# Lightning attention into a SwiGLU block: the load of the decay bases moves from the sync queue to GpSimd's queue

## The chip, the cores and the metric

The kernel runs on one core of a Trainium2 chip. The metric is device time in microseconds (us) of one launch; the median of three runs before the change is 216.38 us (216.28 to 216.65).

The engines are named as in the profile: PE is TensorE (PEld its weight loads), DVE is VectorE, ACT is ScalarE, POOL is GpSimd, SP is SyncE. A name with a q (SPq, ACTq) is an engine's own queue of instructions that issue DMA transfers or handle semaphores. Each engine works through its instructions in order, and waits on semaphores that other engines or DMA transfers raise.

## What is computed

Linear attention with a decay per head, over blocks of 64 positions, and then a SwiGLU feed-forward block on the result. Shapes: q, k and v are 4 x 8 x 768 x 64 (batch, heads, sequence, head size), lam has 8 values (one decay base per head), the weights are 512 x 1536 twice and 1536 x 512.

```python
def _attn_ref(q, k, v, lam):
    ...
    Dmask = np.where(rel >= 0, lam[:, None, None] ** rel[None, :, :], 0.0)
    lam_pow = lam[:, None, None] ** (pos[None, :, None] + 1)
    lam_block = lam ** block
    ...
    for b in range(nb):
        ...
        intra = np.einsum('bhic,bhjc->bhij', qb, kb) * Dmask[None]
        intra = np.einsum('bhij,bhjd->bhid', intra, vb)
        inter = np.einsum('bhid,bhde->bhie', qb * lam_pow[None], kv_state)
        out[:, :, sl] = intra + inter
        ...
        kv_state = lam_block[None, :, None, None] * kv_state + np.einsum('bhsd,bhse->bhde', kb_dec, vb)

def _moe_ref(x, w_gate, w_val, w_out):
    g = x @ w_gate
    silu = g * (1.0 / (1.0 + np.exp(-g)))
    val = x @ w_val
    return silu * val @ w_out
```

## The kernel before

The work is cut into 12 groups. A group is one batch entry and 256 positions of all 8 heads; two groups make one of six column tiles of the feed-forward part. Per group the kernel loads k, q and v, casts k and q to bf16, transposes them, forms scores, masks them, and multiplies with v; a state per batch entry is carried on. The feed-forward part takes gate and value products over twelve slices of the hidden size (`ffn_gate`, `ffn_val`), and then the output product. The order of all instructions on each engine is written out by hand (`manual_schedule`); a plan attaches the attention work of later groups to steps of the feed-forward loop. So the first two groups stand alone at the head of the kernel, and from the first `ffn_gate` on PE has feed-forward products to work on.

What matters here is the head. The decay bases enter as follows:

- Line 137 loads lam into `lam_row`, one partition of 8 values, as the first transfer of the sync queue.
- Lines 138 to 143 load groups 0 and 1, through `load_fp32` (line 115): k and q in halves of 4 heads (256 KB each), taken in turn, then v in halves. All go to the sync queue, but for the two halves of q of group 0, which ACT's queue issues. After them the sync queue issues the first weights (`w_piece`, line 241).
- On POOL, `make_identity`, two position tables (`irow`, line 159, and `ipos`, line 164) and the causal masks (lines 168 to 179) are built.
- On PE, four filler products into an unused bank (line 188) are followed by line 189, a product of a row of ones with `lam_row`, which puts lam on all 128 partitions. Four more fillers follow (line 154, called at line 190), and then the transposes.
- ACT takes the logarithm of that (lines 201 and 203); DVE multiplies it with `ipos` (line 205), and ACT makes the tables of decays for the queries (`qdec_table`, line 209) before and between its casts of k (line 306), and exponentiates DVE's product (line 945). The casts of q of group 0 are on DVE (line 306 too).
- POOL scales v with these decays (`v_scale`, line 266), and casts a part of group 1.
- Masked scores are made at line 369 on DVE after the score products (line 362) on PE; line 324 (ACT) and line 328 (DVE) take the transposed k and q out of their banks, q with its decays multiplied in.

In the text, k0a and k0b are the two halves of k of group 0, k1a and k1b those of group 1, and q and v likewise.

```python
lam_ps = bank()
b = bank()
for _ in range(4):
    nc.tensor.matmul(b, warm[:, 0:128], warm, start=True, stop=True)
nc.tensor.matmul(lam_ps[:, 0:H], ones[:, 0:128], lam_row, start=True, stop=True)
warm_up(4)
```

Of the kernel before, what the change touches and what calls it, by code (L numbers as in the profile page):

```python
# [19 lines left out]
@with_exitstack  # L20
def kernel(
    ctx: ExitStack,
    tc: tile.TileContext,
    q: bass.AP,
    k: bass.AP,
    v: bass.AP,
    lam: bass.AP,
    moe_w_gate: bass.AP,
    moe_w_val: bass.AP,
    moe_w_out: bass.AP,  # L30
    out: bass.AP,
):
    nc = tc.nc
    with tc.manual_schedule():
        _body(ctx, tc, nc, q, k, v, lam, moe_w_gate, moe_w_val, moe_w_out, out)


def _body(ctx, tc, nc, q, k, v, lam, moe_w_gate, moe_w_val, moe_w_out, out):
    B, H, S, D = q.shape
# [94 lines left out]
                                ap=[[D, n], [-S * D if rev else S * D, H], [1, D]]))  # L134

    lam_row = const.tile([1, H], FP32, name="lam_row")
    nc.sync.dma_start(out=lam_row, in_=bass.AP(tensor=lam.tensor, offset=lam.offset, ap=[[0, 1], [1, H]]))
    for g in range(2):
        for c in range(2):
            load_fp32(g, nc.sync, k, "kraw", c * H // 2, (c + 1) * H // 2)  # L140
# [1149 lines left out]
```

## Time and profile before

| | |
|---|---|
| median of the runs | 216.38 us |
| span of the profiled execution | 215.0 us |
| PE busy | 208.1 us (97%) |
| DVE, ACT, POOL busy | 148.3, 130.9, 92.7 us |
| DMA: moved, mean rate | 39.76 MB, 185 GB/s |
| DMA in the first 14 us | 3.97 MB, 284 GB/s |

The span goes from the first to the last instruction of one profiled execution; the time of a run has some more around it. Busy time is the time in which an engine's instructions run, without those that only issue transfers or handle semaphores. A DMA transfer has two times: that of its issue, which is an instruction of a queue, and that until its data have landed. The profile gives the second only as a figure per group of issues.

The transfers of the first 14 us, as the profile's list of issues has them: the halves of k, q and v are 256 KB, with 4.5, 3.6 (ACT's queue) or 4.5 (SP's), and 4.7 us as the median from issue to landing; for `lam_row` it gives no time to landing.

### The profile page before, as it was taken

What the parts mean: (1) busy time and instruction counts of PE and PEld (TensorE: products, weight loads), DVE (VectorE), ACT (ScalarE), POOL (GpSimd) and SP (SyncE); (2) the same over time, 40 slices, a digit from 0 to 9 for tenths busy, and PEclk for the clock granted to TensorE, in tenths of its full rate; (3) what the DMA queues carried; (4) which work ended last, traced back from release to release, by engine and by line L of the source; (5) the groups of instructions that cost most, each with busy time, mean ns of one, the idle gap of its engine ahead of it and who ended that gap; (6) DMA issues with size and microseconds to landing.
All of it is one profiled execution on the core that took longest, in us unless ns stands there. A gap on an engine that the chain in (4) does not pass through costs nothing.

```text
span 215.0 us, 6856 instructions
## 1 busy us (share of the span) xinstructions
PE 208.1 (97%) x2797; PEld 153.3 (71%) x2801; DVE 148.3 (69%) x267; ACT 130.9 (61%) x280; POOL 92.7 (43%) x128
## 2 busy tenths in 40 slices
PE   8789999999999999999999999999999999999993
PEld 3467445887888548866754545888888888888883
DVE  1773447576677989874569878697988389961940
ACT  5878676756636153638369487774983676636522
POOL 6675755818399440595962153240750022200200
PEclk9999999999999999999999999999999999999999
DMA  6999999999999778899576859855000500005014
GB/s 188 345 354 381 376 336 296 285 226 223 309 387 174 185 212 208 244 214 263 122 198 143 217 121 257 207 121 201 5 3 5 195 0 3 0 0 198 0 52 146
DMA packets 82176, 39.76 MB, mean 185 GB/s; under 512 B 45410, under 2 KB 77794, under 8 KB 82146
## 3 DMA queue, kind: packets, MB, share of 16 engines
q1 hardware_dynamic: 80946, 38.74, 64.7%
q10 hardware_dynamic: 1200, 0.59, 0.9%
q8 instruction: 22, 0.36, 0.7%
q14 instruction: 8, 0.07, 0.1%
HBM read 28.31 MB, written 6.29 MB: 161 GB/s over the span
## 4 chain that ended last, share of the span: by engine, by line
PE 93%; DMA 2%; DVE 1%; SPq 1%; ACT 0%; issue 0%; DVEq 0%
PE bank L823 22%; PE bank L585 20%; PE bank L603 19%; PE bank L733 17%; PE bank L623 5%; PE bank L531 3%; DMA kraw<-in_k_dram 2%; PE bank L518 2%; PE bank L424 2%; PE bank L362 1%; DVE ssb L369 1%; SPq L115 1%; PE bank L392 1%; PE bank L322 1%; ACT qk L306 0%
## 5 line engine op out<-in xcount | busy, mean ns | idle before, releaser
L607 DVE TENSOR_TENSOR h<-sil,bank 128x256 bf16<-128x256 bf16 (+1 forms) x67 | 35.0, 533 | 29.9 <-PE bank L603 17.2
L585 PE MATMUL bank<-xt,wg_sb 128*128 128x256 bf16 (+1 forms) x276 | 52.8, 315 | 0.0
L603 PE MATMUL bank<-xt,wv_sb 128*128 128x256 bf16 (+1 forms) x276 | 52.5, 314 | 0.0
L590 ACT ACTIVATE sil<-bank 128x256 bf16<-128x256 f32 (+1 forms) x67 | 31.6, 481 | 21.8 <-PE bank L585 18.4
L603 PEld LDWEIGHTS <-wv_sb 128*128 128x128 bf16 x276 | 26.9, 98 | 14.8 <-POOL wv_sb L249 0.2
L585 PEld LDWEIGHTS <-wg_sb 128*128 128x128 bf16 x276 | 25.9, 98 | 13.6 <-issue 0.2
L266 POOL TENSOR_TENSOR v_s<-v,dec 128x512 bf16<-128x512 f32 (+1 forms) x18 | 23.0, 1295 | 24.3 <-DMA v<-in_v_dram 17.3
L763 POOL TENSOR_TENSOR h<-sil,es 128x512 bf16<-128x512 bf16 x6 | 7.0, 1165 | 47.4 <-ACT sil L760 47.4
L823 PEld LDWEIGHTS <-h 128*128 128x128 bf16 x240 | 23.3, 98 | 3.4 <-issue 0.3
L823 PE MATMUL bank<-wo_sb,h 128*128 128x256 bf16 x180 | 21.5, 273 | 0.0
L823 PEld LDWEIGHTS <-hs 128*128 128x128 bf16 x180 | 17.6, 98 | 2.7
L369 DVE TENSOR_TENSOR ssb<-bank,causal 128x512 bf16<-128x512 f32 x24 | 15.4, 684 | 1.8 <-PE bank L362 1.8
L479 POOL TENSOR_TENSOR kvf<-kvs,ups 128x256 f32<-128x256 f32 x8 | 6.5, 814 | 20.9 <-ACT ups L446 20.9
L733 PEld LDWEIGHTS <-ws 128*128 128x128 bf16 x144 | 13.8, 98 | 1.8
L823 PE MATMUL bank<-wt,hs 128*128 128x256 bf16 x120 | 15.0, 273 | 0.0
L775 DVE TENSOR_TENSOR bank<-bank,es 128x512 f32<-128x512 f32 x12 | 7.8, 694 | 9.6 <-PE bank L733 9.6
L479 POOL TENSOR_TENSOR kvf<-kvf,ups 128x256 f32<-128x256 f32 x16 | 13.0, 815 | 0.9
L760 ACT ACTIVATE sil<-bank 128x512 bf16<-128x512 f32 x18 | 10.5, 596 | 3.7 <-PE bank L733 3.7
L733 PE MATMUL bank<-xs,ws 128*128 128x256 bf16 x96 | 12.6, 273 | 0.0
L763 DVE TENSOR_TENSOR h<-sil,bank 128x512 bf16<-128x512 bf16 x18 | 11.8, 683 | 0.3 <-ACT sil L760 0.3
L623 PE MATMUL bank<-wo_sb,h 128*128 128x512 bf16 x45 | 10.7, 380 | 0.2
L733 PE MATMUL bank<-xt,wg_sb 128*128 128x256 bf16 x72 | 10.8, 273 | 0.0
(119 smaller groups left out, 360.3 us busy)
## 6 DMA issues: line engine op xcount, KB each, us to landing
out_dram<-osb SPq DMA_DIRECT2D x22, 256.0 KB, 2.6
v<-in_v_dram SPq DMA_DIRECT2D x18, 256.0 KB, 4.6
woraw<-in_moe_w_out_dram SPq DMA_DIRECT2D x6, 512.0 KB, 7.1
kraw<-in_k_dram SPq DMA_DIRECT2D x24, 128.0 KB, 3.4
qraw<-in_q_dram SPq DMA_DIRECT2D x24, 128.0 KB, 3.4
wraw<-in_moe_w_gate_dram SPq DMA_DIRECT2D x5, 512.0 KB, 6.9
wraw<-in_moe_w_val_dram SPq DMA_DIRECT2D x5, 512.0 KB, 7.0
kraw<-in_k_dram SPq DMA_DIRECT2D x4, 512.0 KB, 6.3
```

The source lines that it names most:

```text
L266: eng.tensor_tensor(out=st[("vs", g)][:, h0:h1], in0=st[("v", g)][:, h0:h1].rearrange("p h (s d) -> p h s d", s=2), in1=vfac(g, h0, h1), o ...
L369: nc.vector.tensor_tensor(out=ssb[:, h2, 2 * c:2 * c + 2].rearrange("p a s n -> p a (s n)"), in0=sp[(c, h2)].rearrange("p (a x) -> p a x", ...
L479: nc.gpsimd.tensor_tensor(out=o, in0=f, in1=u, op=ALU.add)
L585: nc.tensor.matmul(gp[:, n0:n1], wg_sb[:, mc, fs], xt[:, g0:g1, mc].rearrange("p g b n -> p g (b n)"), start=(mc == 0 and n0 == 0), stop=( ...
L590: nc.scalar.activation(sil[:, 0:N], gp[:, 0:N], AF.Silu)
L603: nc.tensor.matmul(vp[:, n0:n1], wv_sb[:, mc, fs], xt[:, g0:g1, mc].rearrange("p g b n -> p g (b n)"), start=(mc == 0 and n0 == 0), stop=( ...
L607: nc.vector.tensor_tensor(out=h_sb[:, fc % FH, b0:b1].rearrange("p b n -> p (b n)"), in0=sil[:, 0:N], in1=vp[:, 0:N], op=ALU.mult)
L623: nc.tensor.matmul(ps, st[("h", t, fc // FH)][:, fc % FH, b], wo_sb[:, fc, c0:c1], start=(fc == 0), stop=(fc == FC - 1))
L733: nc.tensor.matmul(o[:, fi * 256:fi * 256 + 256], lhs(i, c, 2 * j + fi), rhs(c), start=(start and fi == 0 and c == 0), stop=(c == KH - 1), ...
L760: nc.scalar.activation(sil[key], src, AF.Silu)
L763: eng.tensor_tensor(out=h_of(half, r), in0=v3(sil[half, r]), in1=v3(src), op=ALU.mult)
L823: nc.tensor.matmul(o, lhs(f), rhs(f), start=(start and f == 0), stop=(f == FH - 1), skip_group_check=True)
```

## The change

One word: the load of `lam_row` is issued by GpSimd in place of the sync engine.

```diff
     lam_row = const.tile([1, H], FP32, name="lam_row")
-    nc.sync.dma_start(out=lam_row, in_=bass.AP(tensor=lam.tensor, offset=lam.offset, ap=[[0, 1], [1, H]]))
+    nc.gpsimd.dma_start(out=lam_row, in_=bass.AP(tensor=lam.tensor, offset=lam.offset, ap=[[0, 1], [1, H]]))
```

On POOL the new issue stands ahead of the memset of the identity, the first instruction of the kernel proper there. The sync queue begins with k0a. The number and order of the instructions on PE, DVE and ACT stay as they are.

## The prediction

> **What bounds the kernel now.** I read the page's busy table and slices first, then the chain of waits over the first 30 us, then the timelines of ACT and POOL there, then stretches of DMA rate.
>
> ```profile
> PE 208.1 (97%) x2797; PEld 153.3 (71%) x2801; DVE 148.3 (69%) x267; ACT 130.9 (61%) x280; POOL 92.7 (43%) x128
> PE   8789999999999999999999999999999999999993
> ```
>
> TensorE has work almost all the time; the only slices with holes are the first four, so a change to the loads at the start can move the end only by moving the moment when TensorE becomes solid. From there on everything shifts as a block. The chain of waits (start, length, what):
>
> ```profile
> 0.81 0.35 SPq L137
> 1.16 0.06 issue
> 1.22 0.42 SPq L115
> ...
> 3.33 5.23 DMA kraw<-in_k_dram
> 8.56 0.02 issue
> 8.58 0.63 ACT qk L306
> ...
> 14.72 0.64 PE bank L531 x31
> 15.36 0.54 PE bank L585 x4
> ```
>
> By this chain the head is the SP queue's issues one after another, lam first, then the transfer of the first half of group 1's k (k1a below; q1a, v0a and so on likewise), then its cast on ACT, from which the transposes, scores and masks run to 14.72 and the gate matmuls at 15.36. Lam costs SP 0.35 + 0.06 = 0.41 us there. But a chain shows one path only; ACT's timeline (start, length, engine, line; in brackets the idle time before and its releaser) shows the second:
>
> ```profile
> 3.27 0.18 ACT L201 ACTIVATE ln_lam<-bank 128x8 f32<-128x8 f32 x1 [0.16 <-PE bank L189]
> 3.77 0.91 ACT L209 ACTIVATE qdec<-irow,lnp 128x256 bf16<-128x256 f32 x2
> 4.88 0.62 ACT L306 CAST qk<-kraw 128x512 bf16<-128x512 f32 x1 [0.20 <-DMA kraw<-in_k_dram]
> 7.80 0.57 ACT L324 COPY qkt<-bank 128x512 bf16<-128x512 bf16 x1
> 8.58 0.62 ACT L306 CAST qk<-kraw 128x512 bf16<-128x512 f32 x1 [0.21 <-DMA kraw<-in_k_dram]
> ```
>
> Lam goes through the matmul L189 (start 2.64, when the four fillers of L188 are through; 0.59 long), the logarithms, two exponentials (to 4.68) and only then comes the first cast of k. ACT waited for k only 0.20 at 4.88 and 0.21 at 8.58. So the lam path runs beside the k path with 0.41 us to spare, once L189 is pushed off 2.64.
>
> How early lam lands today: the semaphore event of L189 in the timeline of its line stands at 2.0.
>
> ```profile
> L189 PEldq EVENT_SEMAPHORE  x1: 51/51/51, 2.0 to 2.0; - x1
> 0.80 0.20 POOL masks.py:197 MEMSET ident<- 128x128 bf16 x1 [0.29 <-POOLq L1274]
> 7.23 2.05 POOL L266 TENSOR_TENSOR v_s<-v,dec 128x512 bf16<-128x512 f32 x2 [2.96 <-ACT qk L306]
> ```
>
> If that event is lam's (L189 waits for lam and for the ones of L150, which were there at 1.06), lam needs 1.2 us from its issue at 0.81, 0.84 of it after the 0.35 of issuing, on DMA engines that were still empty. In any case it was there by 2.64. The two POOL lines (start, length) show where the new issue goes, ahead of the identity at 0.80, and how much idle time POOL has before 7.23.
>
> **The change, part by part.**
>
> SP loses one issue: all later issues may start 0.41 earlier. How much of that becomes data is read from the DMA engines (columns of busy time, then clock, DMA share, GB/s):
>
> ```profile
> 2.00:2.50 0.50, 0.50 (x2) 0.00 (x0) 0.00 (x0) 0.50 (x1) 0.50 (x4) 1.00 0.48 108
> 2.50:3.00 0.50, 0.50 (x3) 0.36 (x2) 0.00 (x0) 0.50 (x1) 0.45 (x3) 1.00 0.99 295
> 5.00:5.50 0.50, 0.24 (x4) 0.01 (x1) 0.00 (x0) 0.50 (x2) 0.00 (x0) 1.00 1.15 345
> ```
>
> Full rate is 345 GB/s. In 2.0 to 2.5 the engines are half empty, as only ACT's q is flowing: 0.5 x (345 - 108) = 118 KB missing, 0.34 us at full rate. With k beside q from the start that hole can be filled; after it the engines are full and SP issues at their pace (q1a's issue took 1.70, the next ones come every 0.74 us, 256 KB each, 354 GB/s), so nothing more comes of the 0.41. k1a can land 0 to 0.41 earlier; I take 0.34. q1a also loses its wait for lam's semaphore, which had long passed at 3.88: nothing.
>
> ACT's side allows that much: k0a lands earlier too, the 0.20 of waiting goes, and the rest follows, so ACT is ready for k1a at 8.38 - 0.20 = 8.18, against 8.56 - 0.34 = 8.22 for k1a. The gain with lam in time is therefore 0.34: 216.38 - 0.34 = 216.04.
>
> POOL gains one issue before its tables. The trace has no transfer issued by POOL. Bounds of the issue: 0.35, what SP needs for the same one, and 2.05, the pair of v scalings, as the longest stretch POOL spends on one thing in the head. POOL casts 128x512 f32 in 0.61 where DVE takes 0.43, so POOL is the slower engine for like work and I go above SP: 1.05, one 128x512 scaling. The delay on POOL costs nothing by itself: identity (done 1.37, used 4.74), irow (1.70, used 3.77), ipos (2.06, used 3.55), masks (4.28, used 7.16) each stand an added 1.05; ipos would be late from 1.49 on, and then by the excess, into L205 and the q cast behind it on DVE. POOL's own next work is at 7.23.
>
> Lam's landing, L: 0.80 + issue + flight. Flight is 0.84 on empty engines. Now the engines fill from 2.0 on with k and q. What landing under load adds: from 2.00 to 8.56 they moved 320 GB/s x 6.56 = 2.10 MB, while k1a and all issued before it are 7 x 0.262 = 1.835 MB, so k1a landed some 0.77 after the last byte that it could wait for (an estimate from these rows). I take the whole of it, because lam arrives when both queues are full: L = 0.80 + 1.05 + 0.84 + 0.77 = 3.46, and 0.05 for the semaphore event: 3.5. Bounds: 0.80 + 0.35 + 0.84 = 2.0 (as today), and 0.80 + 5.2 = 6.0, if lam took as long as k1a's 5.23.
>
> What is queued behind the wait: on PE, L189 is followed by the four fillers of L154 (1.75) and by the first transposes; ACT's L201, L203 and L209 hold the first k cast behind them; DVE's L205 holds the cast of q0a. All of them move by 3.5 - 2.64 = 0.86. Of this 0.20 goes into ACT's wait for k0a and 0.21 into that for k1a; the rest, 0.45, is on the path: ACT reaches k1a at 8.38 + 0.66 = 9.04 instead of 8.58. DVE's masks have the same slack (0.46 idle ahead of L328 at 10.68). That k1a lands 0.34 earlier is then worth nothing.
>
> **Sum.** The profiled execution's span is 215.0, 1.4 below the median of the runs, 216.38; this difference stays. +0.45 on the span: 215.45; on the median 216.83, and I say 216.85, +0.2%. A change below 0.2% (0.43 us) can't be told from none, and this forecast sits at that edge: L = 3.47 is the point where it is passed.
>
> **The rivals.**
>
> Covered (not slower): lam lands before 2.8, as in 2.0 plus some tenths, L189 starts within 0.2 of 2.64 and the filled hole brings 0.34: 216.04. For it: L has 0.6 us behind the fillers of L188 today. Against it: one instruction more on a slower engine and full DMA engines. It decides while L is below 2.64 + 0.41 - 0.34 = 2.7 fully, and up to 3.05 in part. The Trainium skill (DMA: Bandwidth & Descriptors, Latency and other measured facts) gives the first byte of a transfer issued by GpSimd at about 1 us and by the sync queue at about 0.6, so 0.4 later; added to 2.05 this would be L = 2.45, hidden, and the time 216.04. No run so far shows it; the page's figure says nothing of full engines.
>
> Wash: L between 2.8 and 3.45, or k1a not earlier because its engines are full anyway: between -0.2 and +0.4, say 216.4.
>
> Clock (slower still): 512-wide fillers start 0.43 apart at L188 and L154 (3.16 to 4.42) though the granted clock reads 1.00, and the same width later takes 0.216 (L585, four in 0.86); PE turned fast near 4.7, after 3.9 us of nearly unbroken work. With a hole of 0.8 us between L188 and L189 this may come later. On the path between 5.56 and 7.60 PE has L322 (0.40), L362 (0.42) and L322 (0.62); at half rate at most 1.44 more, of which I take 1.0: 217.85. It decides if the hole is enough to put off the fast state. Against it: PE stays fast from 5 to 9 with far larger holes. The Trainium skill (TensorE: Matmul & The Clock Gate, Part 1) says that the clock opens after one busy window of about 3.4 us that runs freely, not with the kernel; by it a hole of 0.8 in one window may or may not count.
>
> More than the hole: k1a earlier by the full 0.41 and by the thin 2.5 to 3.0 as well (0.07): 215.9, faster by over 0.2%. It needs lam before 2.7 and ACT ready at 8.1.
>
> **How the numbers follow.** Lam late by POOL's issue and full engines, with 0.43 or more lost: 0.40; its own range is 216.6 to 217.5 (L from 3.3 to 4.2). Clock: 0.10. Wash: 0.22. Covered: 0.20. More than the hole: 0.08. So slower 0.50, same 0.42, faster 0.08. The range reaches from 216.0 (covered) to 217.9 (clock); L above 4.5, and the fast rival, are left out.
>
> **What would show it.** In the new trace: SP's first k issue at about 0.81; the 2.0 to 2.5 stretch near 300 GB/s; L189 starting well after 2.7 with PE idle before it (right), or at 2.64 (covered); ACT's idle time before L306 gone at 4.9 and 8.6 and L306 starting near 9.0; POOL's tables about 1 us later with no one waiting; fillers of L154 and transposes at the old spacing (clock wrong). The forecast falls if L189 still starts at 2.64, or if k1a's cast starts before 8.5.

## The result, and the profile after

The changed kernel takes 222.12 us (median of six; the kernel before 216.36 us beside it), and the ratio is 1.0237, interval 1.0206 to 1.0269. A second set gave 221.57 against 216.41, 1.025 (1.0214 to 1.0287). Slower, as forecast, but by some 5 us where 0.45 was forecast, and outside the range. One of the twelve executions of the two sets had a mean granted clock (the share of full speed that TensorE was given) of 0.57 and took 359.85 us; the ratios leave it out, and what is shown below comes from an undisturbed one, whose span is 219.5 us against 215.0 before.

The page of the changed kernel, busy times and TensorE's slices:

```profile
PE 208.9 (95%) x2797; PEld 154.3 (70%) x2801; DVE 149.0 (68%) x267; ACT 130.8 (60%) x280; POOL 91.6 (42%) x129
...
PE   3986999999999999999999999999999999999993
```

The busy times are the same within 1.1 us; TensorE's slices differ in the first four alone, the first and the fourth having larger holes. So the place to read is the head again. The chain of waits of the changed kernel over the first 24 us (start, length, what):

```profile
1.31 4.51 DMA lam_row<-in_lam_dram
5.82 0.14 issue
5.96 0.56 PE bank L189 x2
6.51 1.82 PE bank L154 x4
8.33 0.43 PE bank L322 x4
...
11.97 0.63 ACT qk L306
...
16.82 1.30 DVE ssb L369 x2
18.12 1.24 issue
19.36 0.64 PE bank L531 x31
20.00 0.54 PE bank L585 x4
```

Before, this chain ran through SP's issues and k1a. Now it begins with lam's transfer, and everything in the head hangs on it: L189 starts at 5.96 instead of 2.64 (+3.32), and by the chain the gate matmuls of L585 at 20.00 instead of 15.36 (+4.64). The span grew by 4.5, so the rest of the kernel moved nearly as a block. Two parts make up the 4.64: the masks (L369) end 3.40 later (18.12 instead of 14.72), and then PE stands for 1.24 us more, marked issue. ACT's timeline of the changed kernel (idle time before and its releaser in brackets):

```profile
6.55 0.18 ACT L201 ACTIVATE ln_lam<-bank 128x8 f32<-128x8 f32 x1 [3.32 <-PE bank L189]
...
7.06 0.91 ACT L209 ACTIVATE qdec<-irow,lnp 128x256 bf16<-128x256 f32 x2
7.87 0.60 ACT L306 CAST qk<-kraw 128x512 bf16<-128x512 f32 x1
...
9.44 0.58 ACT L324 COPY qkt<-bank 128x512 bf16<-128x512 bf16 x1 [0.71 <-PE bank L322]
...
11.97 0.62 ACT L306 CAST qk<-kraw 128x512 bf16<-128x512 f32 x1
```

ACT sits 3.32 us for lam. No cast waits for k any more: the first is at 7.87 instead of 4.88, the third (k1a) at 11.97 instead of 8.58. The two waits of 0.20 and 0.21 are gone, but the lag behind the old times is larger at L324 (3.45) and k1a (3.39) than at the start (3.32).

### The profile page after: what moved, and what is told of

It reads as the page before. It is cut to its first block, busy times and chain, and to the rows that moved or that the text cites. A ratio compares the mean times of both kernels' runs of the same rounds, so it can differ in the third digit from the quotient of the medians.

```text
span 358.1 us, 6860 instructions
## 1 busy us (share of the span) xinstructions
PE 349.3 (98%) x2801; PEld 204.2 (57%) x2801; DVE 151.4 (42%) x267; ACT 135.9 (38%) x280; POOL 92.2 (26%) x129
## 4 chain that ended last, share of the span: by engine, by line
PE 96%; DMA 1%; ACT 1%; DVE 1%; issue 0%; POOLq 0%; DVEq 0%
PE bank L823 23%; PE bank L603 21%; PE bank L585 21%; PE bank L733 18%; PE bank L623 5%; PE bank L531 2%; PE bank L518 1%; DMA lam_row<-in_lam_dram 1%; PE bank L424 1%; PE bank L322 1%; PE bank L362 1%; PE bank L392 1%; DVE ssb L369 1%; PE bank L154 1%; ACT qkt L324 0%
## 5 line engine op out<-in xcount | busy, mean ns | idle before, releaser
L603 PE MATMUL bank<-xt,wv_sb 128*128 128x256 bf16 (+1 forms) x276 | 86.6, 465 | 0.0
L585 PE MATMUL bank<-xt,wg_sb 128*128 128x256 bf16 (+1 forms) x276 | 85.7, 458 | 0.0
L603 PEld LDWEIGHTS <-wv_sb 128*128 128x128 bf16 x276 | 36.1, 131 | 37.6 <-issue 27.3
L585 PEld LDWEIGHTS <-wg_sb 128*128 128x128 bf16 x276 | 34.8, 129 | 32.8 <-issue 22.3
L823 PEld LDWEIGHTS <-h 128*128 128x128 bf16 x240 | 31.2, 131 | 15.1 <-issue 0.9
L823 PE MATMUL bank<-wo_sb,h 128*128 128x256 bf16 x180 | 36.7, 388 | 0.0
L823 PE MATMUL bank<-wt,hs 128*128 128x256 bf16 x120 | 25.4, 390 | 0.0
L733 PEld LDWEIGHTS <-ws 128*128 128x128 bf16 x144 | 18.2, 128 | 8.5
L733 PE MATMUL bank<-xs,ws 128*128 128x256 bf16 x96 | 20.8, 387 | 0.0
L623 PE MATMUL bank<-wo_sb,h 128*128 128x512 bf16 x48 | 18.9, 580 | 0.0
L369 DVE TENSOR_TENSOR ssb<-bank,causal 128x512 bf16<-128x512 f32 x24 | 15.5, 685 | 7.5 <-PE bank L362 7.5
L733 PE MATMUL bank<-xt,wv_sb 128*128 128x256 bf16 x72 | 17.4, 387 | 0.0
L733 PEld LDWEIGHTS <-wv_sb 128*128 128x128 bf16 x96 | 13.0, 135 | 5.6
```

What stands on the lines that cost most here:

```text
L369: nc.vector.tensor_tensor(out=ssb[:, h2, 2 * c:2 * c + 2].rearrange("p a s n -> p a (s n)"), in0=sp[(c, h2)].rearrange("p (a x) -> p a x", ...
L585: nc.tensor.matmul(gp[:, n0:n1], wg_sb[:, mc, fs], xt[:, g0:g1, mc].rearrange("p g b n -> p g (b n)"), start=(mc == 0 and n0 == 0), stop=( ...
L603: nc.tensor.matmul(vp[:, n0:n1], wv_sb[:, mc, fs], xt[:, g0:g1, mc].rearrange("p g b n -> p g (b n)"), start=(mc == 0 and n0 == 0), stop=( ...
L623: nc.tensor.matmul(ps, st[("h", t, fc // FH)][:, fc % FH, b], wo_sb[:, fc, c0:c1], start=(fc == 0), stop=(fc == FC - 1))
L733: nc.tensor.matmul(o[:, fi * 256:fi * 256 + 256], lhs(i, c, 2 * j + fi), rhs(c), start=(start and fi == 0 and c == 0), stop=(c == KH - 1), ...
L823: nc.tensor.matmul(o, lhs(f), rhs(f), start=(start and f == 0), stop=(f == FH - 1), skip_group_check=True)
```

## The experiments

Ratios are to the kernel before, run in the same set, with 95% intervals. The code cuts are shortened: `in_=lam` stands for the full access pattern of lam, which is the same everywhere.

**How late lam lands, and why.** Two kernels leave lam on SP and only put it further back.

```diff
 lam_second: SP issues k0a, lam, k0b, v0a, ...
 lam_late_sp: SP issues k0a, k0b, v0a, v0b, lam, k1a, ...
```

> SP issues k0a first and lam second, so lam is issued near 1.3, the moment of POOL's issue in the changed kernel, but by SP. Theory 'load': a full ring ahead of it makes lam late for SP too, with L189 near 4 to 6 and a time of 219 to 222. Theory 'POOL's path': lam lands by 3, and the time is that of no_lam, 217.5 to 218.5.

> SP issues lam too, but after k and v of group 0: a late lam without POOL. It lands 3 us or more after its issue near 2.9, as it is queued behind full engines. Theory 'late lam': the time follows the landing alone, whoever issues it: landing at 5.8 gives 221 to 222, at 5.0 about 0.8 less. Theory 'POOL': below 218.

Measured: 218.9 us, 1.0124 (1.0097 to 1.015), and 224.3 us, 1.035 (1.0319 to 1.0382). In each, SP's issue of lam and the semaphore event of the product with lam (it is at line 190 there); lam_second first:

```profile
1.33 0.38 SPq L141 DMA_DIRECT2D lam_row<-in_lam_dram  x1
...
L190 PEldq EVENT_SEMAPHORE  x1: 51/51/51, 4.6 to 4.6; - x1
```

```profile
2.96 0.44 SPq L144 DMA_DIRECT2D lam_row<-in_lam_dram  x1
...
L190 PEldq EVENT_SEMAPHORE  x1: 51/51/51, 7.8 to 7.8; - x1
```

The same 32 bytes on the same queue take 1.2 us as the first transfer (0.81 to 2.0, the kernel before), 3.3 behind one half of k (1.33 to 4.6), and 4.8 behind four halves (2.96 to 7.8), with q of group 0 on ACT's queue beside them each time. The time grows with the moment at which the product with lam starts, whoever issues lam: 4.75 goes with 1.24%, 5.96 (the changed kernel) with 2.4%, 7.91 with 3.5%. But not all of that is lam. The chains, lam_second first, where the masks end at 16.93, and then lam_late_sp, where they end at 19.82:

```profile
16.93 0.14 issue
17.06 0.64 PE bank L532 x31
17.70 0.54 PE bank L586 x4
```

```profile
19.82 1.24 issue
21.06 0.64 PE bank L532 x31
```

With the product 2.11, 3.32 and 5.27 us later than before, the masks end 2.21, 3.40 and 5.10 later: that is lam. The 1.24 marked issue in the changed kernel and in lam_late_sp comes on top, and lam_second does not have it; it is taken up below.

**What POOL's path adds.** One look at the kernel before with four more loads of lam into an unused tile, one from POOL and one from SP in a loaded stretch (336 GB/s from 27.6 to 33.3 us), and one from each late in the kernel. POOL's late one was issued at 143.9, ahead of the still stretch that was meant: the engines were idle when it began, but moved 284 to 291 GB/s from 144.4 to 145.9.

```diff
+at(s0[4], lambda: nc.gpsimd.dma_start(out=pad[0:1, 0:8], in_=lam))
+at(s0[5], lambda: nc.sync.dma_start(out=pad[0:1, 8:16], in_=lam))
...
+nc.gpsimd.dma_start(out=pad[0:1, 16:24], in_=lam)
...
+nc.sync.dma_start(out=pad[0:1, 24:32], in_=lam)
```

> The kernel before with four more loads of the 8 values of lam into the unused tile pad: one by POOL and one by SP while the engines run full (24 to 35 us), one by POOL and one by SP late, where they move 3 to 5 GB/s (about 150 to 165 us). Theory 'load': the landing time goes by the load of the engines: POOL's late one lands in under 2.5 us from its issue, as SP's 1.2 at the start, and in the full stretch both need 4 us or more. Theory 'POOL's path': POOL's transfers need 4 us in both places, SP's 1 to 2 in both.

POOL's two issues (duration in ns, start), then issue to landing in the loaded stretch and late:

```profile
L1053 POOL DMA_DIRECT2D pad<-in_lam_dram x1: 702/702/702, 27.6 to 27.6; - x1
...
L1236 POOL DMA_DIRECT2D pad<-in_lam_dram x1: 566/566/566, 143.9 to 143.9; - x1
```

```profile
pad<-in_lam_dram POOLq DMA_DIRECT2D x1, 0.0 KB, 5.7
...
pad<-in_lam_dram POOLq DMA_DIRECT2D x1, 0.0 KB, 3.1
```

5.7 us loaded and 3.1 late, so 3.1 is not the time on idle engines. The view names no landing for SP's two, but the trace's packet records have their 32 bytes: they moved 3.4 us after the start of their issue in the loaded stretch (29.84 to 33.19), 2.1 late (147.11 to 149.16), and 0.9 at the start of the kernel (0.81 to 1.70). POOL's last packets moved 5.3 and 2.7 after theirs. So the load makes both issuers' transfers later.

In the changed kernel POOL's issue and lam_second's begin at the same moment (1.31, 1.33); POOL's lands at 5.82, lam_second's at 4.62. So of lam's 3.8 us of delay (2.0 to 5.82) some 2.6 are what lam_second has too (0.5 of later start and 2.1 behind the transfers ahead), and some 1.2 are POOL's path, 0.3 of it the longer issue (0.70 against 0.38). This rests on one pair of traces, and the load differs a little: SP issues k0b at 1.33 in the changed kernel and at 1.76 in lam_second. What the other 0.9 consists of is open; the traces show that POOL's load is moved as 32 packets, the first at 4.80 and the last at 5.30, where SP's 32 bytes in lam_second are one packet, at 4.09. The Trainium skill (DMA: Bandwidth & Descriptors, Latency and other measured facts) gives 0.4 between the first bytes of the two issuers; I had weighed that as the difference between their landings, and the 1.2 found here, under load, is larger. The same section says that HBM access goes from 0.2 us on average to 2 us at high load; the 2.6 between POOL's two transfers go the same way, but neither of them ran on idle engines throughout.

**POOL's issue alone.** The kernel before, with SP's lam kept and a load by POOL added: first into a new 32-byte tile, then into an unused part of the tile of ones, so that no other tile moves. A third kernel has a new 32-byte tile and no load.

```diff
+lam_spare = const.tile([1, H], FP32, name="lam_spare")               # pool_spare
+nc.gpsimd.dma_start(out=lam_spare, in_=lam)
...
+nc.gpsimd.dma_start(out=ones_t[0:1, 128:136], in_=lam)               # pool_spare2
...
+shift = const.tile([1, H], FP32, name="shift")                       # shift32, ahead of lam_row
+nc.vector.memset(shift, 0.0)
```

> The kernel before, with lam still loaded by SP, and one more transfer of the same 8 values issued by POOL at the same place into a spare tile that nobody reads: POOL's own delay without the late lam. Theory 'late lam': 216.4, within 0.3. If POOL's tables or its later work decide: 217 or more.

> As pool_spare, but the spare transfer goes into an unused part of the tile of ones, so that no tile moves to another address. pool_spare had shifted all tiles by 32 bytes and its load rate at the start was 290 GB/s in place of 345. Theory 'shift': without it 216.4, within 0.4, since POOL's own 1.2 us of delay is covered. Theory 'POOL queue': a transfer of POOL's queue beside the others slows them all, and 228 comes again.

> The kernel before with one tile of 32 bytes allocated ahead of lam_row (and filled by DVE): the shift alone, no transfer by POOL. Theory 'shift': 228, and 290 GB/s in the first slices. Theory 'POOL queue': 216.4.

Measured: 228.7 us, 1.0561 (1.0531 to 1.0591); 216.54 us, 0.9996 (0.9972 to 1.002); 228.91 us, 1.0558 (1.0517 to 1.0599). POOL's issue costs nothing, as forecast, and what made pool_spare slow is the place of the other tiles: 32 bytes further on, the loads are slower, in shift32 without any load by POOL. The stretch 4 to 8 us before, and in shift32 (busy time of PE, PEld, DVE, ACT, POOL, then clock, DMA share, GB/s):

```profile
4.00:8.00 4.00, 3.27 (x40) 1.71 (x38) 1.76 (x6) 3.56 (x10) 1.04 (x2) 1.00 1.14 342
```

```profile
4.00:8.00 4.00, 3.96 (x40) 2.09 (x38) 1.77 (x5) 3.22 (x9) 0.47 (x2) 1.00 1.17 293
```

342 against 293 GB/s, with the DMA engines as busy (1.14 and 1.17). Why the place matters was not looked into. So an experiment that adds a tile here has to keep the others where they are.

**What SP's head start is worth.** Lam's load taken away (the lam values are a constant there, so the decays of the reference are not computed); the same with SP first loading lam's 8 values to an unused place; lam ahead of q on ACT's queue; and lam alone on ACT's queue with q and k in turn on SP's.

```diff
-nc.sync.dma_start(out=lam_row, in_=lam)
+nc.vector.memset(lam_row, 0.98)                                      # no_lam, no_lam_sp
+nc.sync.dma_start(out=ones_t[0:1, 128:136], in_=lam)                 # no_lam_sp
...
+nc.scalar.dma_start(out=lam_row, in_=lam)                            # lam_act, one_queue
...
+if g == 0: load_fp32(g, nc.sync, q, "qraw", ...)                     # one_queue, ahead of k
```

> The load of lam is left out: lam_row is filled with the constant 0.98 by DVE, so the decays are not those of the input. SP begins with k as in the changed kernel, and lam is never late: the pure gain of the freed issue. By the prediction 216.0 (0.34 less); if the DMA engines are full anyway, 216.4.

> lam_row is the constant 0.98 as in no_lam, so the decays are not those of the input, and SP begins with a load of the same 8 values into an unused place that nobody reads: the 0.41 us ahead of k0a are back. If k's earlier start is what cost no_lam 1.6 us: 216.4, as the kernel before. If it was the constant or the filling by DVE: 218.0 again.

> lam is loaded by ACT's queue ahead of q, and SP begins with k0a: what the change wanted, without POOL. lam is in time (2.0), but q0a starts 0.41 later and k0a 0.41 earlier than before. If the order in which q and k land decides: no better than no_lam, 217.5 to 219. If k0a first is a gain: 216.0.

> lam is issued by ACT's queue, alone there, and SP issues q0a, k0a, q0b, k0b, v and so on in one row, so that each half lands by itself in place of q and k sharing the engines. no_lam has shown that k's earlier start put off q0a's cast from 3.75 to 4.71. If that sharing is what cost no_lam its 1.6 us: 216.0 to 216.4, at most 0.4 below the kernel before. If SP's issues are too slow alone: 217 or more.

Measured: no_lam 218.01 us, 1.0069 (1.0044 to 1.0094); no_lam_sp 216.97, 1.0022 (1.0004 to 1.0039); lam_act 218.26, 1.0111 (1.0073 to 1.0149); one_queue 218.37, 1.0068 (1.0033 to 1.0103); of one_queue only the time is used. With lam out of the way altogether and k issued first, the kernel is slower. The stretches in which the hole was to be filled, in no_lam, and then in the changed kernel:

```profile
2.00:2.50 0.50, 0.50 (x2) 0.00 (x0) 0.00 (x0) 0.50 (x1) 0.50 (x4) 1.00 0.51 114
2.50:3.00 0.50, 0.50 (x3) 0.37 (x2) 0.00 (x0) 0.50 (x1) 0.45 (x3) 1.00 0.45 103
```

```profile
2.00:2.50 0.50, 0.50 (x2) 0.00 (x0) 0.00 (x0) 0.50 (x1) 0.42 (x3) 1.00 0.42 126
2.50:3.00 0.50, 0.21 (x1) 0.00 (x0) 0.00 (x0) 0.50 (x1) 0.50 (x4) 1.00 0.41 123
```

Before, the second stretch had 295 GB/s. The hole was not filled; it became twice as wide: 0.5 x (114 + 103) = 109 KB from 2.0 to 3.0 us where it had been 0.5 x (108 + 295) = 202 KB. With q on ACT's queue and k on SP's issued at the same 0.81, full rate begins half a microsecond later. Who pays first is q0a, whose cast on DVE stood at 3.75 with no wait (the kernel before, then no_lam):

```profile
3.75 0.43 DVE L306 CAST qk<-qraw 128x512 bf16<-128x512 f32 x1
```

```profile
4.71 0.43 DVE L306 CAST qk<-qraw 128x512 bf16<-128x512 f32 x1 [0.93 <-DMA qraw<-in_q_dram]
...
6.23 0.43 DVE L306 CAST qk<-qraw 128x512 bf16<-128x512 f32 x1 [1.09 <-DMA qraw<-in_q_dram]
```

k0a gains 0.3 by it (4.88 to 4.58), q0a loses 0.96, and PE's order has q's transposes first. This is only a part of the 0.7%: k1a's cast is 0.17 later (8.75), the gate by no_lam's chain 0.55 (15.91), with 0.69 marked issue ahead of the last 30 products of L531 on it, and the rest comes after the gate and was not followed. With a small load back ahead of k on SP's queue (no_lam_sp) the rate in 2.5 to 3.0 is 285 again, q0a's cast stands at 3.71, and the loss is 0.2%. lam_act, with its product with lam at 2.64 as before, has its second stretch full (290) and pays in another way: q is issued 0.57 later and its first cast is at 4.88.

**What absorbs the lateness, and the clock.** The changed kernel again, and with fourteen fillers instead of four ahead of the product with lam, so that PE works until lam lands.

```diff
-    for _ in range(4):
+    for _ in range(14):        # after_fill
         nc.tensor.matmul(b, warm[:, 0:128], warm, start=True, stop=True)
```

> The changed kernel once more, for a profile of an undisturbed execution: 221 to 223 us. Theory 'late lam': lam lands near 5.9, L189 starts 3.3 us later than before, 0.4 of this is taken up, so the first cast of group 1's k starts 2.9 us later and the first gate matmuls as well, and some 2.5 us more must be lost elsewhere. Theory 'clock': the 512-wide fillers after L189 and the transposes behind them run at half rate for 3 to 4 us longer than before, and the rest of the 5.5 us is lost there. Theory 'weights': the rest is lost after 15 us, as casts of weights on POOL.

> The changed kernel with 14 fillers ahead of L189 in place of 4, so that PE has no hole while it waits for lam. If the clock theory holds (PE turns fast only after some us without a hole), PE is fast before lam lands, and the time is that of the late landing alone: 216.4 + 2.9 = 219.3. If the hole has no part in it, 221.5 to 222.5 as the changed kernel; up to 0.9 above it if the fillers run at the slow rate to 6.8.

The second took 220.67 us, 1.0209 (1.0168 to 1.025), between the 219.3 and the 221.5 that were expected: the intervals overlap, so the times alone don't tell the two apart. What follows is read from one trace of each. TensorE in the changed kernel, then with fourteen fillers:

```profile
5.96 0.56 PE L189 MATMUL bank<-lam_row,ones 1*128 1x8 f32 x2 [3.25 <-DMA lam_row<-in_lam_dram]
6.45 1.89 PE L154 MATMUL bank<-const-bfloat16-1.0 128*128 128x512 bf16 x4
8.13 0.63 PE L322 MATMUL bank<-ident,qk 128*128 128x128 bf16 x4
...
17.55 0.24 PE L531 MATMUL bank<-ssb,v_s 64*64 64x128 bf16 x1 [0.25 <-issue]
19.36 0.64 PE L531 MATMUL bank<-ssb,v_s 64*64 64x128 bf16 x31 [1.57 <-issue]
```

```profile
0.85 5.29 PE L188 MATMUL bank<-const-bfloat16-1.0 128*128 128x512 bf16 x14 [0.85 <-PEq L1274]
6.07 0.38 PE L189 MATMUL bank<-lam_row,ones 1*128 1x8 f32 x2
6.38 1.05 PE L154 MATMUL bank<-const-bfloat16-1.0 128*128 128x512 bf16 x4
7.39 0.40 PE L322 MATMUL bank<-ident,qk 128*128 128x128 bf16 x4
```

After the hole of 3.25 us the next fillers and transposes run slow (1.89 and 0.63, against 1.05 and 0.40 when the hole is filled), though the granted clock reads 1.00 in the stretches of the changed kernel. A hole of 2.05 (lam_second) has the same sequel, 1.89 and 0.63; whether one of 0.86 would is not shown. Nor is PE fast from 4.7 on whenever the hole is missing: in pool_spare2, without a hole, four transposes from 5.49 still take 0.63, at no cost in time. By ACT's timeline the cast of k1a is at 11.18 with the hole filled and at 11.97 without: 0.79 us for the slow products, though lam's product was 0.11 later there. Filled, 3.43 of lateness at L189 arrives as 2.60 at k1a; so slack was there, and the slow products used it up. By the chains the gate starts at 18.32 (+2.96) when filled, at 20.00 when not; the first includes 0.73 of a stop like the one that comes next.

**The idle time marked issue.** In the changed kernel PE stands for 1.57 us after the first of the 32 products of L531 at 17.55, 1.24 of it on the chain, and no engine releases it. A transfer of a queue named instruction falls there (one packet of 16 KB in the DMA view between 17 and 18.2). To tell a fetch of PE's instructions from a wait that belongs to L531, the four fillers behind the product with lam became many narrow ones: the same number of columns in all, but more instructions.

```diff
-    warm_up(4)
+    warm_up(32, 64)     # after_small32, before_small32: 28 matmuls more
+    warm_up(64, 32)     # after_small64: 60 more
```

> The changed kernel, but the four 512-wide fillers behind L189 are 32 of 64 columns: the same columns, 28 matmuls more ahead of everything else on PE. Fetch theory (PE stops for its own instructions after a fixed number of them): the stop moves 28 matmuls up, out of the first matmul of L531 into the first few of L424 at about 16.9, or the fetch, which starts with matmul number 171, now comes that much earlier in the work; the idle 1.57 ahead of L531 at 19.36 is gone or is found elsewhere; if the fetch is now under way while PE waits for ACT or DVE, the gate starts near 18.8, 1.2 earlier, and the time is 220.4. Rival (the stop belongs to L531, by a wait that the profile does not show): L531 is idle before its second matmul as it was, gate at 20.00, time 221.6.

> The same edit in the kernel before. Fetch theory: the stop (idle 0.25 marked issue ahead of L531 at 14.40) moves 28 matmuls up into L424 near 13.5; it was hidden behind the masks, which end 14.72, so the time moves little, by less than 0.2%, unless the stop becomes longer than that cover. Rival: the same picture as before, L531 at 14.40 with issue in front. In both the time stays near 216.4.

> As the first, with 64 fillers of 32 columns: 60 matmuls more. Fetch theory: the stop moves 60 matmuls up, to the matmuls of L322 and L518 near 15.3 to 16.2 of the changed kernel, where PE has its small waits; the gate at 18.3 to 19.0. Rival: L531 as it was, gate at 20.00.

Measured: 222.57 us, 1.0241 (1.0202 to 1.0279); 216.78 us, 0.9998 (0.9969 to 1.0026); 220.34 us, 1.0138 (1.01 to 1.0176). TensorE in after_small32, in before_small32, and in after_small64:

```profile
17.22 0.25 PE L424 MATMUL bank<-v_s,qk 64*64 64x64 bf16 x6
18.54 0.41 PE L424 MATMUL bank<-v_s,qk 64*64 64x64 bf16 x26 [1.07 <-issue]
```

```profile
13.31 0.25 PE L424 MATMUL bank<-v_s,qk 64*64 64x64 bf16 x6
14.01 0.41 PE L424 MATMUL bank<-v_s,qk 64*64 64x64 bf16 x26 [0.45 <-issue]
```

```profile
16.88 0.45 PE L424 MATMUL bank<-v_s,qk 64*64 64x64 bf16 x32
17.57 1.02 PE L531 MATMUL bank<-ssb,v_s 64*64 64x128 bf16 x32 [0.25 <-issue]
18.52 0.61 PE L585 MATMUL bank<-xt,wg_sb 128*128 128x256 bf16 x4
```

With 28 more matmuls the stop sits after six of L424 in both kernels, 27 places ahead of where it was (after 32 of L424 and one of L531); fourteen fillers, ten more, had put it after 24 of L424, 9 places ahead. It follows the number of instructions, not the line, as a wait of PE for its own program would. The packets fit: by the trace's records PE goes on 1.3 to 1.5 us after the packet's end in all of these (18.03 to 19.36 in the changed kernel, 15.75 to 17.17 with fourteen fillers, 17.15 to 18.54 and 12.60 to 14.01 with 28 more matmuls, 19.58 to 21.06 in lam_late_sp). (The 0.25 marked issue ahead of L531 stays where it is in all of them; I had taken it for the stop in the expectation, and it is not.) With 60 more it falls out of the stretch that sets the end, L531 waits for the masks only, the gate starts at 18.59 by its chain, within the 18.3 to 19.0 expected, and the interval of its ratio lies below the changed kernel's. After_small32 was no faster, against the 220.4 expected: its stop moved but stayed on the path (the gate at 20.14), one more batch of transposes ran slow (eight of L322 in 1.03 instead of 0.81), and after its stop the granted clock fell to 0.50 (20.0 to 22.5 us), so that the first four gate products took 0.97 instead of 0.54.

Why the fetch comes late is not settled: in the kernel before and in lam_second its packet starts between PE's 171st and 172nd matmul (12.44, 14.88), in the changed one 1.2 us after the 171st (17.07).

## Why the prediction was right in sign and wrong in size

- Lam late as the main theory: right, the chain begins with it. The step that failed is lam's landing, which was mis-sized. POOL's issue starts at 1.31 rather than 0.80, takes 0.70 (forecast 1.05), and lam lands 4.51 after its start, at 5.82, where 0.80 + 1.05 + 0.84 + 0.77 had put it at 3.5. The flight of 0.84 was that of empty engines; 0.77 for the load was too little: lam_second shows 2.1 for the transfers ahead of it, and POOL's path came to 1.2 more. The upper bound, 6.0 from k1a's 5.23, came nearest, and I left it out of the range.
- "0.41 to spare", and the rival Clock: the slack was there, but Clock came true beside the main theory instead of apart from it. Lam's 3.32 reached k1a's cast as 3.39 with PE's hole open and as 2.60 (of 3.43) with it filled. The slow products cost 0.79 there, near the 1.0 that I had given the rival; but the hole is four times as long as the one forecast (3.25 against 0.86), so the prediction's own case was not tried.
- The gain of 0.34 from a filled hole: wrong in sign. With k beside q from the start the hole in the loads grew instead of filling. Without lam, and thus without any lateness, the kernel loses 0.7%, so the rivals Covered and More than the hole would not have come true even with lam in time. In the changed kernel this loss is hidden, since q0a's cast waits for lam (6.98) longer than for its data.
- POOL's tables late for nothing: right, 0.9996 with POOL's issue alone.
- Not foreseen, and at nothing in the sum: the stop of PE for its instructions, 1.24 on the chain. Where it is moved away (after_small64), the time falls from 221.6 to 220.3. In the kernel before nothing of it can be seen: its packet ends at 13.38, the masks at 14.72, and the rest of L531 starts with them, 1.34 after the packet.
- The sum as it stands: lam's 3.32 less the 0.41 to spare would have been 2.91; the masks end 3.40 later, since the slow products used the slack up (0.49 more), and the stop adds 1.24: +4.64 at the gate, against +4.5 on the span. Two kernels bear the split out: lam_second, without the stop, has its gate at 17.70 (+2.34, for 2.11 at the product), and after_small64 has it at 18.59 (+3.23, for 3.47).

## What to carry to other kernels

A small load that the whole head waits for belongs first on a queue, ahead of the bulk: behind one 256 KB load it took 3.3 us instead of 1.2, which dwarfs the 0.4 us of its issue. It has to be the queue whose bulk can best wait: first on ACT's queue, ahead of q, lam was in time too, and that kernel was still 1.1% slower. When a step on the path is called free to move, price its landing by a transfer that ran under load, not by one on empty engines. And a later head can uncover a stop that other work covers today: where an idle stretch has no releaser, count the instructions ahead of it in both kernels.

## What the runs showed of the hardware that was not expected

- With both queues beginning their bulk loads at 0.81, 93 to 125 KB had moved between 2.0 and 3.0 us (lam_late_sp, no_lam, lam_second, the changed kernel); with one of them beginning 0.4 to 0.6 later, 202 to 203 KB (the kernel before, lam_act, no_lam_sp). Why is open.
- Moving the tiles by 32 bytes takes 14% off the load rate (342 to 293 GB/s) and adds 5.6% to the time.
- PE stops after a fixed number of its instructions (ahead of about the 222nd matmul in the trace's records; the place moved up by 9 and by 27 with 10 and 28 more matmuls ahead), for up to 1.57 us, and resumes 1.3 to 1.5 us after a packet of instructions has ended.
- After such a stop the granted clock can fall: to 0.50 from 20.0 to 22.5 us in after_small32 and to a mean of 0.65 from 21 to 24 us in lam_late_sp, but not in the profiled execution of the changed kernel.
- A load of 32 bytes issued by POOL needs 4.1 us from issue to landing (pool_spare2) and 4.5 (the changed kernel) at the start of the kernel, 5.7 at 336 GB/s, and 3.1 where the engines were idle at first and then moved up to 291 GB/s.
